# Sparse attention and a two-layer MLP on one core: scores and value products issued in runs per half unit, MLP matmuls pinned to their place, and the lower halves of weights subtracted on VectorE while weights are converted

## The chip, the core and the metric

The kernel runs on one core of a Trainium2 chip. The metric is the device time of one execution in microseconds, of which the median of three runs is taken. Five engines work side by side, each through its own list of instructions in order: TensorE (PE, whose weight loads are shown apart as PEld), VectorE (DVE), ScalarE (ACT), GpSimd (POOL) and SyncE (SP, here only an issuer of transfers).

## The reference

Three layers follow each other. Attention runs over 4 batches and 8 heads of 576 positions and 64 channels, where the first four heads see the last 32 positions and the others every 32nd position. Its output, 2304 tokens by 512, goes through an MLP with 2048 hidden units. The result is routed to eight experts of 288 tokens each by a greedy choice over all logits, and each expert is an MLP with 1024 hidden units.

```python
scores = scale * np.matmul(q, k.transpose(0, 1, 3, 2))
mask_local = (rel >= 0) & (rel < stride)
mask_strided = (rel >= 0) & (pos[None, :] % stride == pos[:, None] % stride)
attn = np.exp(scores - max); attn = attn / (attn.sum(-1) + 1e-09)
x = (attn @ v).transpose(0, 2, 1, 3).reshape(B * S, H * D)
...
h = x @ w_in
x = np.maximum(0.01 * h, h) @ w_out
...
logits = x @ w_gate        # greedy: each token one expert, each expert 288 tokens
out[mask] = np.maximum(x[mask] @ w1[e], 0.0) @ w2[e]
```

The weights `w_in` and `w_out` come as 64-bit floats and are made 32-bit on the chip.

## The kernel before

**Attention.** A unit is one batch and two heads; there are 16, each handled in two half units (`seq`, 32 in all). One turn of the loop in `attention()` works on three half units at once: the scores of the newest (`a_qk`, L147), the transposes of the weights of the one two turns older (`a_pt`, L185, in two parts), and the value products of the one three turns older (`a_pv`, L201); it also transposes q and k of the next unit (`a_tr`, L114). Two or three tiles make a half unit. The scores of a tile are two matmuls, one per head, each over 64 rows of the array (the two heads lie on different rows); the value products of a tile are two matmuls, each into 64 columns. A matmul of 32-bit floats shows as two records in the trace, so one tile of scores is an `x4` in a timeline.

**MLP.** Tokens are taken in six blocks of 384. A step `n` is one block and one of 16 slices of the hidden units. `g1` (L367) makes 12 matmuls of 384 columns, `g2` (L389) nine of 512 columns for the step before. Products of 32-bit floats are made from an upper and a lower half: `split` (L345) copies the weight slice into `hi`, and `lo` is the difference. In the matmuls `hi`/`lo` appear as operands of L374 to L376 and L398 to L400. The hidden values go through ScalarE (L382), VectorE (L383), ScalarE (L384) and VectorE (L385). The one bank `p1` that `g1` writes has a single buffer, so the first matmul of the next step (L374) waits until L383 has read it.

**Conversion.** `convert` (L313) turns a 512 KB piece of a 64-bit weight into 32 bits: ScalarE (L321), then three VectorE instructions (L323, L324, L325). The pieces are loaded from GpSimd's queue (L307, L310) into two buffers, each of which is loaded again when L325 has read it. There are 32 pieces, two per step of the first block.

**Order.** Each of the three is a Python generator; a `yield` marks where another may go on. `mlp()` asks before each step for what it needs: `2n + 3` converted pieces, and `DONE` half units of attention (8 for the first block, 16 for the second). Between its own yields, attention is advanced by a credit:

```python
            credit += 0.9 if DONE[0] < 16 else 0      # first 16 steps
        elif st < 64:
            credit += 0.5 if DONE[0] < 32 else 0
        ...
        while credit >= 1:
            next(A, None)
            credit -= 1
```

A list scheduler then orders each engine's instructions. It follows the program order as a priority and may move an instruction ahead; one on which `tc.keep_in_program_order` is called stays behind all that was written before it on its engine. In the kernel before, that call (`pin`) is used only in the expert part.

After step 47 three blocks have their second product left. These, the routing and the experts follow; the change does not touch them.

Of the kernel before, what the change touches and what calls it, by code (L numbers as in the profile page):

```python
# [26 lines left out]
def body(ctx, tc, q, k, v, w_in, w_out, w_gate, w1, w2, out):  # L27
# [119 lines left out]
    def a_qk(u, g):  # L147
        nq, nk, tl = group(u, g)
        n = len(tl)
        tag = "p2" if u < 5 and g else "pS"  # L150
        p = [ps.tile([128, 4, 128], F32, name=f"pS{h}", tag=tag, bufs=BUFS[tag]) for h in range(2)]
        s = at.tile([126, 2, 3, 128], F32, name="sc", tag="sc", bufs=3)
        mx = at.tile([126, 3, 2, 3], F32, name="mx", tag="mx", bufs=4)
        SC[u, g] = s, mx

        def score(i, m):
            for h in range(2):
                nc.vector.tensor_tensor_reduce(s[:nq, h, i, :nk], p[h][:nq, i, :nk], m[:nq, :nk], -0.125,  # L158
                                               3.0e38, OP.add, OP.min, mx[:nq, 0, h, i:i + 1])
                nc.scalar.activation(s[:nq, h, i, :nk], s[:nq, h, i, :nk], AF.Exp,  # L160
                                     bias=mx[:nq, 0, h, i:i + 1], scale=-1.0,
                                     accum_out=mx[:nq, 1, h, i:i + 1])

        for i, (q0, k0, m, _) in enumerate(tl):
            for h in range(2):
                r = slice(64 * h, 64 * h + 64)
                nc.tensor.matmul(p[h][:nq, i, :nk], QK[u][r, 0, 32 + q0:32 + q0 + nq],
                                 QK[u][r, 1, k0:k0 + nk], start=True, stop=True)
            if u < 2 and i:
                nc.tensor.matmul(p[0][:, 3], ident, QK[u][:, 0, 32:160], start=True, stop=True)  # L170
            yield
        for i, t in enumerate(tl):
            score(i, t[2])

# [10 lines left out]
    def a_pt(u, g, h):  # L185
        nq, nk, tl = group(u, g)
        n = len(tl)
        if h == 0:
            PT[u, g] = at.tile([128, 2, 3, 128], F32, name="pt", tag="pt")
        tag = "p2" if u < 5 and h else "pT"  # L190
        p = ps.tile([128, 4, 128], F32, name="pP", tag=tag, bufs=BUFS[tag])
        for _ in range(3 if u < 5 else 0):
            nc.tensor.matmul(p[:, 3], ident, ident, start=True, stop=True)
        for i in range(n):
            nc.tensor.transpose(p[:nk, i, :nq], SC[u, g][0][:nq, h, i, :nk], ident[:nq, :nq])
        if h or EARLY[0]:
            nc.scalar.activation(PT[u, g][:nk, h, :n, :nq], p[:nk, :n, :nq], AF.Copy)
        else:
            nc.vector.tensor_copy(PT[u, g][:nk, h, :n, :nq], p[:nk, :n, :nq])

    def a_pv(u, g):  # L201
        b, c = divmod(u, 4)
        nq, nk, tl = group(u, g)
        n = len(tl)
        t = PT.pop((u, g))
        tag = "p1" if u < 2 else "pT"
        p = ps.tile([128, 3 * 126], F32, name="pX", tag=tag, bufs=BUFS[tag])
        for i, tt in enumerate(tl):
            for h in range(2):
                nc.tensor.matmul(p[64 * h:64 * h + 64, i * nq:i * nq + nq], VT[u][:nk, tt[3], h, :],  # L210
                                 t[:nk, h, i, :nq], start=True, stop=True)
            if i == 0:
                yield
        pieces = []
        if c < 2:
            s0 = b * S + 288 * g
            o = 0
            while o < 288:
                j, a0 = divmod(s0 + o, BLK)
                w = min(288 - o, BLK - a0)  # L220
                pieces.append((p[:, o:o + w], *(x[:, c, a0:a0 + w] for x in xtile(j))))
                o += w
        else:
            r0, nr = 14 * g, n * nq // 18
            i0 = 0
            while i0 < 18:
                j, a0 = divmod(b * S + 32 * i0, BLK)
                i1 = min(18, i0 + (BLK - a0) // 32)
                pieces.append((p[:, :n * nq].rearrange("p (r i) -> p r i", i=18)[:, :, i0:i1],
                               *(x[:, c, a0:a0 + 32 * (i1 - i0)].rearrange("p (i r) -> p r i", r=32)[:, r0:r0 + nr]  # L230
                                 for x in xtile(j))))
                i0 = i1
        for src, dh, dl in pieces:
            (nc.scalar.copy if u else nc.vector.tensor_copy)(dh, src)
            nc.vector.tensor_sub(dl, src, dh.bitcast(F32))  # L235
# [4 lines left out]
    def attention():  # L240
# [9 lines left out]
        for s in range(n + 3):  # L250
            cur, mid, old = (seq[x] if 0 <= x < n else None for x in (s, s - 2, s - 3))
            u, g = cur or (99, 0)
            A = a_qk(u, g) if cur else iter(())
            V = a_pv(*old) if old else iter(())
            if u + 1 < 16 and s >= 1:
                a_tr(u + 1, g)
                yield
# [5 lines left out]
                yield  # L263
            if cur:
                next(A, None)
                yield
            if old:
                next(V)
                yield
            if u + 1 < 16 and g == 1:  # L270
                a_tr(u + 1, 2)
                yield
            if cur:
                next(A, None)
                yield
            if mid:
                a_pt(*mid, 1)
                yield
            for _ in A:
                pass  # L280
            if s < 1:
                a_tr(u + 1, g)
                yield
            if cur:
                a_norm(u, g)
            for _ in V:
                pass
            if old:
                DONE[0] += 1
            yield  # L290
            if g == 0 and u + 2 < 16:
                a_load(u + 2)
                v_load(u + 2)
# [51 lines left out]
    def split(pool, src, tag, n):  # L345
# [4 lines left out]
            nc.scalar.activation(hi, src, AF.Copy)  # L350
        else:
            nc.vector.tensor_copy(hi, src)  # L352
        nc.gpsimd.tensor_sub(lo, src, hi.bitcast(F32))  # L353
        return hi, lo


# [1 line left out]
    nc.gpsimd.memset(WB, 0.0)  # L358
    L = consts.tile([128, 18, 8], F32, name="L")
    SI, SO, GG, P2 = {}, {}, {}, {}  # L360

    def prep(n):

# [3 lines left out]
    def g1(n):  # L367
# [3 lines left out]
        p1 = ps.tile([128, BLK], F32, name="p1", tag="p1", bufs=1)  # L371
        for c in range(4):
            cs = slice(128 * c, 128 * c + 128)
            nc.tensor.matmul(p1, wh[:, cs], xh[:, c], start=(c == 0), stop=False)  # L374
            nc.tensor.matmul(p1, wh[:, cs], xl[:, c], start=False, stop=False)  # L375
            nc.tensor.matmul(p1, wl[:, cs], xh[:, c], start=False, stop=(c == 3))  # L376
            if c < 3:
                yield
# [10 lines left out]
    def g2(n):  # L389
# [5 lines left out]
        p2 = P2[blk]  # L395
        for t in range(3):
            s = slice(128 * t, 128 * t + 128)
            nc.tensor.matmul(p2[t], gh[:, s], oh, start=(f == 0), stop=False)  # L398
            nc.tensor.matmul(p2[t], gh[:, s], ol, start=False, stop=False)
            nc.tensor.matmul(p2[t], gl[:, s], oh, start=False, stop=(f == 15))  # L400
            if f == 15:
# [128 lines left out]
    A, Cv = attention(), conversion()  # L530
    bg = []
    for n, _ in enumerate(A):
        if n % 10 == 0:
            next(Cv, None)
        if DONE[0] >= 8:
            break
    credit = 0.0
    for n, _ in enumerate(mlp()):
# [3 lines left out]
        if st < 16:  # L542
            if n == 0:
                next(Cv, None)
            credit += 0.9 if DONE[0] < 16 else 0
        elif st < 64:
            credit += 0.5 if DONE[0] < 32 else 0
        if n == 20:
            for a in range(4):
                nc.sync.dma_start(WB[32 * a:32 * a + 32, :, 8 * a:8 * a + 8], w_gate.rearrange("(b j) e -> j b e", j=32))  # L550
# [138 lines left out]
            return f  # L689

    soon = Soon()

    def pin(x):

        tc.keep_in_program_order(x[0] if isinstance(x, tuple) else x)

    def search():

# [367 lines left out]
```

## Time and profile before

| | |
|---|---|
| time, median of 3 runs | 898.53 us (898.48 to 899.33) |
| the profiled execution | 891.85 us, of which 890.1 us is the span from first to last instruction |
| mean granted clock of TensorE | 0.978 of full speed |
| PE busy | 842.4 us (95% of the span) |
| DVE busy | 544.8 us (61%) |
| ACT busy | 441.5 us (50%) |
| POOL busy | 492.1 us (55%) |

The busy shares are averages over stages that differ. Three stretches matter here: up to 72.9 us attention runs almost alone; from 72.9 to 184.3 us steps 1 to 15 of the MLP run beside attention and conversion; from 184.3 to 374 us steps 16 to 47 run beside the rest of attention. PEclk is the granted share of TensorE's clock (1.00 is 2.4 GHz, 0.50 is 1.2 GHz).

### The profile page before, as it was taken

What the parts mean: (1) busy time and instruction counts of PE and PEld (TensorE: products, weight loads), DVE (VectorE), ACT (ScalarE), POOL (GpSimd) and SP (SyncE); (2) the same over time, 40 slices, a digit from 0 to 9 for tenths busy, and PEclk for the clock granted to TensorE, in tenths of its full rate; (3) what the DMA queues carried; (4) which work ended last, traced back from release to release, by engine and by line L of the source; (5) the groups of instructions that cost most, each with busy time, mean ns of one, the idle gap of its engine ahead of it and who ended that gap; (6) DMA issues with size and microseconds to landing.
All of it is one profiled execution on the core that took longest, in us unless ns stands there. A gap on an engine that the chain in (4) does not pass through costs nothing. (4 is left out here: it accounts for less than half of the span.)

```text
span 890.1 us, 17029 instructions
## 1 busy us (share of the span) xinstructions
PE 842.4 (95%) x6272; PEld 710.9 (80%) x6272; DVE 544.8 (61%) x1552; ACT 441.5 (50%) x1098; POOL 492.1 (55%) x402
## 2 busy tenths in 40 slices
PE   8799999899999999999999999997999999999994
PEld 5677766677777787788989777775899999899994
DVE  5787888865546565475645546454758878772320
ACT  5787667464546455444555323332544444444641
POOL 2655646564555565544645355575648547558731
PEclk8999989999999999999999999999899999999998
DMA  8587554420122000044000004362546445546510
GB/s 193 145 199 175 143 137 137 129 63 14 29 46 79 17 6 10 1 160 160 1 1 1 19 1 166 109 205 92 166 147 192 147 133 182 173 146 206 181 52 27
DMA packets 95411, 93.18 MB, mean 105 GB/s; under 512 B 66144, under 2 KB 74336, under 8 KB 95328
## 3 DMA queue, kind: packets, MB, share of 16 engines
q1 hardware_dynamic: 87648, 65.88, 26.0%
q0 software_dynamic: 7680, 26.22, 9.6%
q8 instruction: 49, 0.80, 0.4%
q14 instruction: 34, 0.28, 0.1%
HBM read 76.35 MB, written 15.73 MB: 103 GB/s over the span
## 5 line engine op out<-in xcount | busy, mean ns | idle before, releaser
L353 POOL TENSOR_TENSOR lo<-WI,hi 128x512 fp32r<-128x512 f32 x96 | 127.5, 1328 | 98.9 <-DVE hi L352 58.2
L353 POOL TENSOR_TENSOR lo<-WO,hi 128x512 fp32r<-128x512 f32 x96 | 125.9, 1312 | 88.3 <-ACT hi L350 88.1
L859 POOL TENSOR_TENSOR wlo<-raw,whi 128x1024 fp32r<-128x1024 f32 x48 | 116.8, 2445 | 26.7 <-ACT whi L858 21.7
L350 ACT ACTIVATE hi<-WO 128x512 fp32r<-128x512 f32 x96 | 60.6, 631 | 101.3 <-PE q L961 49.2
L374 PE MATMUL p<-xh,hi 128*128 128x384 f32 x192 | 75.7, 395 | 5.3 <-DVE g L383 5.3
L916 PE MATMUL g<-hh,whi 128*128 128x288 f32 x256 | 78.8, 308 | 0.4 <-DVE exl L879 0.4
L893 PE MATMUL g<-exh,whi 128*128 128x288 f32 x256 | 78.6, 308 | 0.0
L894 PE MATMUL g<-exl,whi 128*128 128x288 f32 x256 | 76.8, 301 | 0.0
L917 PE MATMUL g<-hl,whi 128*128 128x288 f32 x256 | 76.2, 298 | 0.4 <-DVE hl L901 0.4
L895 PE MATMUL g<-exh,wlo 128*128 128x288 f32 x256 | 76.3, 298 | 0.0
L918 PE MATMUL g<-hh,wlo 128*128 128x288 f32 x256 | 75.7, 296 | 0.0
L160 ACT ACTIVATE sc<-sc,mx 96x128 f32<-96x128 f32 (+2 forms) x176 | 67.6, 388 | 15.0 <-DVE mx L158 15.0
L858 ACT ACTIVATE whi<-raw 128x1024 fp32r<-128x1024 f32 x64 | 67.3, 1053 | 2.9 <-DMA raw<-in_moe_w_dram 2.9
L376 PE MATMUL p<-xh,lo 128*128 128x384 f32 x192 | 66.3, 345 | 1.4 <-POOL lo L353 1.2
L421 PE MATMUL p<-xh,hi 128*128 128x384 f32 x192 | 66.4, 346 | 0.0
L375 PE MATMUL p<-xl,hi 128*128 128x384 f32 x192 | 65.8, 343 | 0.2 <-DVE xl L235 0.2
L423 PE MATMUL p<-xh,lo 128*128 128x384 f32 x192 | 64.7, 337 | 0.7 <-POOL lo L353 0.7
L398 PE MATMUL p<-hi,gh 128*128 128x512 f32 x144 | 64.3, 446 | 0.7 <-ACT gh L384 0.7
L422 PE MATMUL p<-xl,hi 128*128 128x384 f32 x192 | 64.4, 335 | 0.0
L182 POOL TENSOR_TENSOR sc<-sc,mx 96x384 f32<-96x384 f32 (+2 forms) x64 | 52.2, 832 | 21.4 <-DVE mx L180 15.2
L932 POOL DMA_INDIRECT out_dram<-o,idx x24 | 24.3, 1011 | 70.4 <-ACT o L908 58.4
L400 PE MATMUL p<-hi,gl 128*128 128x512 f32 x144 | 57.4, 398 | 0.0
(210 smaller groups left out, 2294.3 us busy)
## 6 DMA issues: line engine op xcount, KB each, us to landing
raw<-in_moe_w_dram SPq DMA_DIRECT2D x64, 512.0 KB
wraw<-in_moe_w_in_dram POOLq DMA_DIRECT2D x16, 512.0 KB
wraw<-in_moe_w_out_dram POOLq DMA_DIRECT2D x16, 512.0 KB
g<-g3d SPq DMA_DIRECT2D x16, 384.0 KB
rawq<-in_q_dram SPq DMA_DIRECT2D x32, 144.0 KB
rawk<-in_k_dram SPq DMA_DIRECT2D x32, 144.0 KB
x2d<-x SPq DMA_DIRECT2D x18, 256.0 KB
g3d<-gh SPq DMA_DIRECT2D x16, 192.0 KB
```

The source lines that it names most:

```text
L160: nc.scalar.activation(s[:nq, h, i, :nk], s[:nq, h, i, :nk], AF.Exp, bias=mx[:nq, 0, h, i:i + 1], scale=-1.0, accum_out=mx[:nq, 1, h, i:i ...
L353: nc.gpsimd.tensor_sub(lo, src, hi.bitcast(F32))
L374: nc.tensor.matmul(p1, wh[:, cs], xh[:, c], start=(c == 0), stop=False)
L421: nc.tensor.matmul(p1, wh[:, cs], xh[:, c], start=(c == 0), stop=False)
L858: pin(nc.scalar.activation(hi, raw, AF.Copy))
L859: pin((nc.vector if n in (5, 7) else nc.gpsimd).tensor_sub(lo, raw, hi.bitcast(F32)))
L893: nc.tensor.matmul(p, wh, xh[:, c], start=(c == 0), stop=False)
L894: nc.tensor.matmul(p, wh, xl[:, c], start=False, stop=False)
L895: nc.tensor.matmul(p, wl, xh[:, c], start=False, stop=(c == 3))
L916: nc.tensor.matmul(p, wh, hh[:, j], start=(j == 0), stop=False)
L917: nc.tensor.matmul(p, wh, hl[:, j], start=False, stop=False)
L918: nc.tensor.matmul(p, wl, hh[:, j], start=False, stop=(j == 7))
```

## The change

In `a_qk` the `yield` after each tile of scores goes: one turn issues the scores of all tiles of a half unit in one go. In `a_pv` the `yield` after the first tile goes as well, so all its value products come in one go. The loop of `attention()` loses the yields between these parts: from 8 or 9 per turn it comes to 5 or 6, and the credits are scaled with that (0.9 to 0.6, 0.5 to 0.33), as is the rate of conversions ahead of the MLP (every 10th yield to every 6th). `pin` is moved up and called on the first matmul of each group of three in `g1` and `g2`. The lower half in `split` is subtracted on VectorE until the last piece is converted (`CONV[0] > 31`), and on GpSimd after. The banks tagged `p2` are lent to attention for units 0 to 3 rather than 0 to 4.

```diff
@@ a_qk
-        tag = "p2" if u < 5 and g else "pS"
+        tag = "p2" if u < 4 and g else "pS"
...
             if u < 2 and i:
                 nc.tensor.matmul(p[0][:, 3], ident, QK[u][:, 0, 32:160], start=True, stop=True)
-            yield
+        yield
         for i, t in enumerate(tl):
             score(i, t[2])
@@ a_pt
-        tag = "p2" if u < 5 and h else "pT"
+        tag = "p2" if u < 4 and h else "pT"
@@ a_pv
-            if i == 0:
-                yield
@@ attention
-            V = a_pv(*old) if old else iter(())
...
             if cur:
                 next(A, None)
-                yield
             if old:
-                next(V)
+                a_pv(*old)
+                DONE[0] += 1
                 yield
...
-            if cur:
-                next(A, None)
-                yield
...
-            for _ in A:
-                pass
...
-            for _ in V:
-                pass
-            if old:
-                DONE[0] += 1
-            yield
@@ split
-        nc.gpsimd.tensor_sub(lo, src, hi.bitcast(F32))
+        (nc.gpsimd if CONV[0] > 31 else nc.vector).tensor_sub(lo, src, hi.bitcast(F32))
@@ g1
-            nc.tensor.matmul(p1, wh[:, cs], xh[:, c], start=(c == 0), stop=False)
+            pin(nc.tensor.matmul(p1, wh[:, cs], xh[:, c], start=(c == 0), stop=False))
@@ g2
-            nc.tensor.matmul(p2[t], gh[:, s], oh, start=(f == 0), stop=False)
+            pin(nc.tensor.matmul(p2[t], gh[:, s], oh, start=(f == 0), stop=False))
@@ body
-        if n % 10 == 0:
+        if n % 6 == 0:
...
-            credit += 0.9 if DONE[0] < 16 else 0
+            credit += 0.6 if DONE[0] < 16 else 0
...
-            credit += 0.5 if DONE[0] < 32 else 0
+            credit += 0.33 if DONE[0] < 32 else 0
```

How this moves instructions is seen in the built order of each engine, which holds no times. On PE, early in the MLP (step 4), the scores of one half unit of the strided heads (three tiles, `pS_1238` and `pS_1239`; written at L167) stand between pieces of `g2` (L398 to L400) in the kernel before:

```order
L167 MATMUL pS_1238<-qk 108x108
L167 MATMUL pS_1239<-qk 108x108
L398 MATMUL p_1056<-hi,gh 128x512
L399 MATMUL p_1056<-lo,gh 128x512
L400 MATMUL p_1056<-hi,gl 128x512
L195 MATMUL pP<-ident,sc 128x96 x3
L398 MATMUL p_1057<-hi,gh 128x512
L399 MATMUL p_1057<-lo,gh 128x512
L400 MATMUL p_1057<-hi,gl 128x512
L167 MATMUL pS_1238<-qk 108x108
L167 MATMUL pS_1239<-qk 108x108
L398 MATMUL p_1058<-hi,gh 128x512
```

In the changed kernel, whose lines past the first edit are 2 to 13 lower (L398 is L389), the same half unit stands so:

```order
L390 MATMUL p_1055<-lo,gh 128x512
L391 MATMUL p_1055<-hi,gl 128x512
L167 MATMUL pS_1251<-qk 108x108
L167 MATMUL pS_1252<-qk 108x108
L167 MATMUL pS_1251<-qk 108x108
L167 MATMUL pS_1252<-qk 108x108
L167 MATMUL pS_1251<-qk 108x108
L167 MATMUL pS_1252<-qk 108x108
L389 MATMUL p_1056<-hi,gh 128x512
```

Two of the three tiles are seen in the first fence, apart from each other, and the third stood later still; the three are now one run.

On PE at the turn to step 3, the value products (L210) of a half unit of the local heads in the kernel before:

```order
L210 MATMUL pX<-pt,vt 64x96 x2
L398 MATMUL p_1057<-hi,gh 128x512
L399 MATMUL p_1057<-lo,gh 128x512
L400 MATMUL p_1057<-hi,gl 128x512
L398 MATMUL p_1058<-hi,gh 128x512
L399 MATMUL p_1058<-lo,gh 128x512
L400 MATMUL p_1058<-hi,gl 128x512
L195 MATMUL pP<-ident,sc 128x96 x3
L374 MATMUL p_1185<-xh,hi 128x384
L375 MATMUL p_1185<-xl,hi 128x384
L376 MATMUL p_1185<-xh,lo 128x384
L210 MATMUL pX<-pt,vt 64x96 x4
```

and in the changed one:

```order
L365 MATMUL p_1176<-xh,hi 128x384
L366 MATMUL p_1176<-xl,hi 128x384
L367 MATMUL p_1176<-xh,lo 128x384
L210 MATMUL pX<-pt,vt 64x96 x6
L365 MATMUL p_1176<-xh,hi 128x384
```

The two matmuls, and the four that stood three groups of matmuls behind them, are one run of six.

On VectorE around the hidden values of step 4 (`g<-p_1286`, L383), the kernel before has conversion (L323 to L325), the hidden values (L383, L385), and attention (L136, L179, L180, L235):

```order
L323 TENSOR_SCALAR cg<-cg 128x512
L324 SCALAR_TENSOR_TENSOR cg<-wraw,cg 128x512
L383 TENSOR_TENSOR g<-p_1286,g 128x384
L325 SCALAR_TENSOR_TENSOR WO<-wraw,cg 128x512
L179 TENSOR_SCALAR mx<-mx 108x6
L136 COPY qk<-pT 128x192
L385 TENSOR_TENSOR gl<-g,gh 128x384
L180 RECIPROCAL mx<-mx 108x6
```

The changed one has at the same place (`g<-p_1279`, now L374; conversion is L310 to L312):

```order
L340 TENSOR_TENSOR lo<-WO,hi 128x512
L311 SCALAR_TENSOR_TENSOR cg<-wraw,cg 128x512
L312 SCALAR_TENSOR_TENSOR WI<-wraw,cg 128x512
L179 TENSOR_SCALAR mx<-mx 108x6
L180 RECIPROCAL mx<-mx 108x6
L233 TENSOR_TENSOR xl<-pX,xh 128x192
L374 TENSOR_TENSOR g<-p_1279,g 128x384
L233 TENSOR_TENSOR xl<-pX,xh 128x96
L340 TENSOR_TENSOR lo<-WI,hi 128x512
L376 TENSOR_TENSOR gl<-g,gh 128x384
L310 TENSOR_SCALAR cg<-cg 128x512
L136 COPY qk<-pT 128x192
```

The lower halves (L340) of `WO` and `WI` have come in, one ahead of the step's hidden values and one behind them. In the whole order 31 of the 192 subtractions of `split` are on VectorE, four of them ahead of the hidden values of step 0; the same place has 12 conversions behind it instead of 10.

## Rows read from the trace of the kernel before

**Rows 1.** Busy time by engine in three stretches, with granted clock and DMA share.

```profile
0.00:72.90 72.90, 61.53 (x520) 48.31 (x520) 51.66 (x224) 52.81 (x195) 36.15 (x51) 0.93 0.75 180
72.90:184.30 111.40, 103.27 (x631) 76.57 (x630) 94.15 (x215) 71.57 (x209) 65.09 (x68) 0.95 0.50 134
184.30:374.00 189.70, 189.70 (x1365) 149.51 (x1365) 103.51 (x338) 99.02 (x299) 104.09 (x93) 1.00 0.12 31
```

**Rows 2.** Matmuls grouped by line and shape, 72.9 to 184.3 us.

```profile
L374 PE MATMUL p<-xh,hi 128*128 128x384 f32 x60 | 25.2, 420 | 5.3 <-DVE g L383 5.3
```

**Rows 3.** Timeline of PE around one tile of scores: start us, length us.

```profile
297.50 0.39 PE L399 MATMUL p<-lo,gh 128*128 128x512 f32 x1
297.73 0.39 PE L400 MATMUL p<-hi,gl 128*128 128x512 f32 x1
298.05 0.46 PE L167 MATMUL pS<-qk 64*96 64x128 f32 x4
298.44 0.50 PE L398 MATMUL p<-hi,gh 128*128 128x512 f32 x1
298.78 0.39 PE L399 MATMUL p<-lo,gh 128*128 128x512 f32 x1
```

**Rows 4.** Timeline of PE, a run of scores ahead of the MLP.

```profile
53.77 1.34 PE L167 MATMUL pS<-qk 64*96 64x128 f32 x20
55.04 0.71 PE L193 MATMUL pP<-ident 128*128 128x128 f32 x4
```

**Rows 5.** Timeline of PE, four tiles' and two tiles' records of value products.

```profile
301.20 0.59 PE L210 MATMUL pX<-pt,vt 108*64 108x108 f32 x8
301.73 0.44 PE L374 MATMUL p<-xh,hi 128*128 128x384 f32 x1
...
309.87 0.39 PE L210 MATMUL pX<-pt,vt 128*64 128x96 f32 x4
310.18 0.50 PE L398 MATMUL p<-hi,gh 128*128 128x512 f32 x1
```

**Rows 6.** VectorE instructions grouped by line and shape, 72.9 to 184.3 us.

```profile
L324 DVE SCALAR_TENSOR_TENSOR cg<-wraw,cg 128x512 int32<-128x512 int32 x22 | 24.3, 1106 | 0.3
L323 DVE TENSOR_SCALAR cg<-cg 128x512 int32<-128x512 int32 x21 | 17.4, 828 | 6.4 <-ACT cg L321 6.4
L325 DVE SCALAR_TENSOR_TENSOR WO<-wraw,cg 128x512 int32<-128x512 int32 x11 | 10.5, 953 | 0.1
...
L325 DVE SCALAR_TENSOR_TENSOR WI<-wraw,cg 128x512 int32<-128x512 int32 x11 | 9.4, 858 | 0.2
```

**Rows 7.** Timeline of all engines around one wait of step 7.

```profile
113.47 0.42 DVE L323 TENSOR_SCALAR cg<-cg 128x512 int32<-128x512 int32 x1
...
113.92 0.69 DVE L324 SCALAR_TENSOR_TENSOR cg<-wraw,cg 128x512 int32<-128x512 int32 x1
...
114.46 1.28 POOL L353 TENSOR_TENSOR lo<-WI,hi 128x512 fp32r<-128x512 f32 x1
114.65 1.64 DVE L325 SCALAR_TENSOR_TENSOR WI<-wraw,cg 128x512 int32<-128x512 int32 x1
...
116.21 0.55 DVE L383 TENSOR_TENSOR g<-p,g 128x384 f32<-128x384 f32 x1
...
116.81 0.44 PE L374 MATMUL p<-xh,hi 128*128 128x384 f32 x1 [1.66 <-DVE g L383]
```

**Rows 8.** GpSimd instructions grouped by line and shape, 72.9 to 184.3 us.

```profile
L353 POOL TENSOR_TENSOR lo<-WI,hi 128x512 fp32r<-128x512 f32 x16 | 22.3, 1397 | 5.9 <-ACT hi L350 5.7
L353 POOL TENSOR_TENSOR lo<-WO,hi 128x512 fp32r<-128x512 f32 x14 | 19.3, 1378 | 4.1 <-ACT hi L350 4.0
L307 POOL DMA_DIRECT2D wraw<-in_moe_w_in_dram x10 | 7.9, 793 | 18.0 <-DVE WI L325 7.1 <-PE pX L210 3.1 <-DVE gl L385 2.7
L182 POOL TENSOR_TENSOR sc<-sc,mx 96x384 f32<-96x384 f32 x8 | 6.4, 824 | 1.8 <-DVE mx L180 1.8
```

**Rows 9.** Waits of PE, 0 to 72.9 us: total us, times, longest us.

```profile
PE pP L193 <- ACT qk L134: 2.2, 2, 1.5
```

More of the change, by code (lines that the diff above doesn't have):

```diff
@@ L360, in body, with pin @@
     SI, SO, GG, P2 = {}, {}, {}, {}
+    def pin(x):
+        tc.keep_in_program_order(x[0] if isinstance(x, tuple) else x)
     def prep(n):
@@ L691, in body @@
     soon = Soon()
-    def pin(x):
-        tc.keep_in_program_order(x[0] if isinstance(x, tuple) else x)
     def search():
```

## The prediction

> **What bounds the kernel now.** I first cut the span into stretches by step and read the busy time of each engine [rows 1]. From 184.3 to 374 us PE is busy for 189.70 of 189.70 us at full clock, and VectorE for 103.51: there PE's own order is the bound, and time taken off PE is time taken off the end. From 72.9 to 184.3 us PE is busy for 103.27 of 111.40 and VectorE for 94.15, the most of the others, and the granted clock is 0.95. This stretch holds 15 steps, since L374 runs four times in each and 60 times in all [rows 2]; it has 7.4 us per step, the next stretch of 32 steps 5.9, though conversion and not matmuls is what the first has more of. PE waits there for VectorE's L383, 5.3 us [rows 2]. In the first 72.9 us VectorE has 51.66 us of work and 21 us idle [rows 1].
>
> Then I asked what a piece of attention costs between matmuls of the MLP. L399 to L400 takes 0.23 us from start to start, and this is what a full matmul of 512 columns holds PE for. Where one tile of scores stands between, L400 to the second matmul behind the tile takes 298.78 - 297.73 = 1.05 us, so the tile costs 1.05 - 2 x 0.23 = 0.59 [rows 3]. Of it some 0.09 is ahead of the tile and 0.11 behind the first matmul after it (0.34 instead of 0.23). In a run, 20 records, which are five tiles, take 55.04 - 53.77 = 1.27 us, or 0.25 a tile [rows 4]. So a break into 64-row matmuls and back costs 0.59 - 0.25 = **0.34 us**, whatever it holds. Value products: two tiles (four records) take 0.31 us to the next matmul, four records more take 0.53, that is 0.22 for what was added [rows 5]; with 0.09 and 0.11 as above, a break costs 0.31 + 0.20 - 0.22 = **0.29 us**.
>
> Last I read why VectorE is so busy. The same L324 takes 0.69 us at 113.92 and 1.11 in the mean of 22; L325 takes 1.64 at 114.65, where GpSimd's L353 runs from 114.46 to 115.74, and VectorE goes on only after that. L383 comes at 116.21, and PE has waited 1.66 us for it [rows 6, 7]. Over the stretch the four groups hold 24.3 + 17.4 + 10.5 + 9.4 = 61.6 us; at 0.69 for L324 and L325 and 0.42 for L323 they would need 44 x 0.69 + 21 x 0.42 = 39.2. So **22.4 us** of VectorE's busy time is standing behind GpSimd.
>
> **The change, part by part.**
>
> *Runs from step 16 on.* By the built orders, scores stand in 32 runs before and 13 after, value products in 32 and 16. That removes 19 x 0.34 + 16 x 0.29 = 11.1 us of PE. Some attention slips here from the steps before 16 (three tiles of scores at 0.25, and transposes): I estimate 1.5 us. PE is the bound, so the end moves by **-9.6 us**. Bounds: if only the 0.11 behind a run is saved, 35 x 0.11 - 1.5 = 2.4; if a tile in a run costs 0.20, 12.
>
> *Runs in steps 1 to 15.* 22 to 9 runs of scores, 15 to 8 of value products: 13 x 0.34 + 7 x 0.29 = 6.4 us less on PE, and the 1.5 that slipped.
>
> *Lower halves on VectorE.* GpSimd loses 16 + 14 subtractions, 22.3 + 19.3 = 41.6 us, and keeps the L182s, 16 in the same view at 0.8 us, or 12.8 [rows 8]. If VectorE stands behind GpSimd in proportion, 22.4 x 41.6 / 54.4 = 17.1 us go. What comes in is 27 subtractions (31 less the four ahead of step 0). No row has one on VectorE. L324 reads two operands of the same 128x512, and without disturbance takes 0.69 [rows 7]; at the top stands 1.64, an L325 behind GpSimd. I take 0.69, since GpSimd has little left to stand behind: 18.6 us in. Two conversions more lie ahead of step 0, 2 x (0.42 + 0.69 + 0.69) = 3.6 us out. VectorE's sum is 94.15 - 17.1 + 18.6 - 3.6 = 92, hardly less than before. What changes is that no instruction ahead of L383 lasts 3 us, and that the pieces' loads, which GpSimd issues between its subtractions, go out earlier; VectorE's L323 waits 6.4 us for what those loads feed [rows 6].
>
> *The stretch.* PE needs 111.40 less 5.3 of waits, less 0.05 x 111.4 = 5.6 of half clock, less 6.4 and 1.5: 92.6 us, as much as VectorE. Two engines at 92 that wait for each other don't reach 92. VectorE is busy for 85% now; with its idle of 17 us cut by the waits for L321 and some others it should come to 89%, which is 103.4 us: **-8 us**. Bounds: at 94% it is 98, or -13; at 80%, if the subtractions wait for ScalarE's `hi` with everything queued behind them (conversion, L383, and so PE), 115, or +4.
>
> *Ahead of step 1.* Two conversions and four subtractions, 3.6 + 2.8 = 6.4 us, enter VectorE's first 72.9 us, which have 21 idle; if that cover is gone, the MLP starts 6.4 us later. Scores reach VectorE one piece earlier. I take **+1 us**, between -2 and +6.
>
> *Pins, credits, banks.* The pin adds no instruction. The credits give 4.2 yields a step at 5.5 a half unit where 6.3 at 8.5 stood, which is 3% faster; attention is not what the end waits for. Attention gives back the `p2` banks one unit earlier, as `g2` wants them. I count these at nothing; what a bad pin would cost is a rival.
>
> *Sum:* -9.6 - 8 + 1 = -16.6 us. The rows come from an execution of 891.85 us, which would become 875. It is 6.7 us under the median of the runs, and I take the difference off the median: 898.53 - 16.6 = **882 us**.
>
> **Rivals.**
>
> *VectorE takes it back.* Its sum in steps 1 to 15 is the same, and the new subtractions wait for `hi` in line. Then the stretch gains nothing, and the start loses 2: 898.5 - 9.6 + 2 = 891. For it: 94 of 111 us are busy already. Against: a quarter of this is standing still, which goes. The Trainium skill (Perfetto Trace Analysis, Optimizing Scalar/DVE Operations) says that moving work between GpSimd and VectorE might not help, as they share a read port. The trace agrees that one stands behind the other [rows 7]; by the rule this case would be the likeliest.
>
> *The stretch becomes PE's.* It falls to 95 us, the clock stays up, -16: 898.5 - 9.6 - 16 = 873. For it: most of PE's waits stand behind blocked instructions. Against: VectorE would need 97%.
>
> *Loads are held up.* VectorE gets 27 more instructions with two operands; if each of the 20 loads that GpSimd issues in the stretch is held up by one of 0.69 us, 13.8 us, of which half is on the path as two buffers alternate, 889. Against: the issue of L307 takes 793 ns in the mean of 10 though VectorE is busy for 85% of that time [rows 1, 8]. The Trainium skill (SBUF — State Buffer, SBUF: two separate sides) says that a transfer issued from GpSimd starves while VectorE holds the shared port in a two-port mode, and has one go from some 620 to some 3100 ns. By that the issues would differ widely; the trace doesn't show it [rows 8].
>
> *The pins cost more than the runs save (slower).* An MLP group can no longer pass an attention piece whose operand is late. Place: the first matmul of a score run, which needs both `pS` banks and the copy of q and k, or of a `pT` piece that needs the bank two pieces back. Where no MLP stands between, such a wait took up to 1.5 us [rows 9]. About 22 half units come after step 0; 16.6 us of gain are gone at 0.75 us for each, and at 1 us the time is 898.5 - 16.6 + 22 = 904. Against: from 184.3 us on PE waits for nothing [rows 1], and two turns of the loop lie between the scores of a half unit and their transposes.
>
> *Breaks don't cost what they seem to* (the runs drain as the tiles did): -2.4 and nothing else, 896.
>
> **Chances.** The forecast 0.49, with its own range 874 to 889; VectorE takes it back 0.20; PE's stretch 0.12; loads 0.04; pins 0.12; breaks 0.03. Below 870 lies half of PE's case, above 896 the pins' and some of VectorE's with a late start: 870 to 896 leaves out some 0.19. A change of under 0.2%, or 1.8 us, is about what a measurement of this kernel can't tell from none. Faster: the first four less 0.04, and breaks: 0.83. Same 0.05, slower 0.12.
>
> **What would show it.** After step 16, PE still busy throughout, 5.6 us or less a step, and score records as x8 and x12. In steps 1 to 15, L324 near 0.7 us in the mean, lower halves on VectorE near 0.69, fewer and shorter waits for L383's counterpart, clock above 0.95. The prediction is wrong if the subtractions wait for ScalarE at length, if step 1 starts past 76 us, or if PE waits inside attention pieces.

## The result, and the profile after

The changed kernel takes **884.33 us** (median of 4 runs, 880.87 to 887.44) where the kernel before takes 898.5 (897.41 to 899.33): ratio 0.9845, interval 0.982 to 0.987. The profiled execution lasted 884.1 us, of which 882.3 us is the span. Lines of kernel.py lie 2 to 13 lower than before: L374 became L365, L383 L374, L324 L311, L353 L340, L321 L308.

Busy time by engine, in the same three stretches as [rows 1] (to step 1, steps 1 to 15, steps 16 to 47; then PE, PEld, VectorE, ScalarE, GpSimd, granted clock, DMA share, GB/s):

```profile
0.00:86.30 86.30, 73.66 (x519) 56.19 (x519) 54.61 (x228) 55.35 (x199) 29.39 (x48) 0.82 0.67 159
86.30:186.40 100.10, 90.02 (x603) 71.79 (x602) 87.93 (x237) 68.65 (x202) 28.84 (x39) 1.00 0.55 142
186.40:367.00 180.60, 180.60 (x1398) 151.58 (x1397) 105.33 (x346) 100.98 (x299) 103.29 (x93) 1.00 0.13 32
```

Step 1 starts at 86.3 us instead of 72.9: **+13.4**. Steps 1 to 15 take 100.1 us instead of 111.4: **-11.3**. Steps 16 to 47 take 180.6, from 184.3 to 374.3 before 190.0: **-9.4**. What follows takes 882.3 - 367.0 = 515.3 instead of 890.1 - 374.3 = 515.8. The sum is -7.8 us, the difference of the two profiled executions.

VectorE's groups in steps 1 to 15, for [rows 6] (busy us, mean ns | idle before them, and what ended it), and PE's first matmul of a group, for [rows 2]:

```profile
L311 DVE SCALAR_TENSOR_TENSOR cg<-wraw,cg 128x512 int32<-128x512 int32 x20 | 16.4, 820 | 0.4
L340 DVE TENSOR_TENSOR lo<-WI,hi 128x512 fp32r<-128x512 f32 x14 | 9.8, 703 | 0.6 <-ACT hi L337 0.5
L340 DVE TENSOR_TENSOR lo<-WO,hi 128x512 fp32r<-128x512 f32 x13 | 9.5, 733 | 0.5 <-ACT hi L337 0.4
L310 DVE TENSOR_SCALAR cg<-cg 128x512 int32<-128x512 int32 x20 | 9.5, 476 | 7.3 <-ACT cg L308 7.3
...
L312 DVE SCALAR_TENSOR_TENSOR WO<-wraw,cg 128x512 int32<-128x512 int32 x10 | 7.3, 730 | 0.1
L312 DVE SCALAR_TENSOR_TENSOR WI<-wraw,cg 128x512 int32<-128x512 int32 x10 | 6.9, 688 | 0.1
...
L365 PE MATMUL p<-xh,hi 128*128 128x384 f32 x60 | 22.8, 381 | 5.7 <-DVE g L374 4.0 <-ACT hi L337 1.7
```

The four conversion groups need 16.4 + 9.5 + 7.3 + 6.9 = 40.1 us where they took 61.6. The 27 lower halves bring 19.3, at 703 and 733 ns. The subtractions hardly wait for ScalarE's `hi`: 0.5 and 0.4 us. PE, though, stands no less in this stretch: 100.10 - 90.02 = 10.1 us where it stood 111.40 - 103.27 = 8.1. Its waits for `g` went only from 5.3 us [rows 2] to 4.0, and 1.7 us for `hi` came in. What fell is its busy time, by 13.3 us, with the granted clock at 1.00 where it was 0.95.

PE around a run of scores and one of value products, both of the steps from 16 on (start, length), for [rows 3, 5]:

```profile
209.61 0.40 PE L391 MATMUL p<-hi,gl 128*128 128x512 f32 x1
209.93 0.71 PE L167 MATMUL pS<-qk 64*126 64x126 f32 x8
210.57 0.50 PE L389 MATMUL p<-hi,gh 128*128 128x512 f32 x1
210.91 0.40 PE L390 MATMUL p<-lo,gh 128*128 128x512 f32 x1
...
214.60 0.39 PE L391 MATMUL p<-hi,gl 128*128 128x512 f32 x1
214.92 0.72 PE L210 MATMUL pX<-pt,vt 128*64 128x96 f32 x12
215.56 0.50 PE L389 MATMUL p<-hi,gh 128*128 128x512 f32 x1
215.90 0.39 PE L390 MATMUL p<-lo,gh 128*128 128x512 f32 x1
```

Two tiles of scores in one run cost 210.91 - 209.61 - 2 x 0.23 = 0.84 us, worked out as for [rows 3]; apart they cost 2 x 0.59 = 1.18. That is 0.34 saved for one break, with tiles of 126 columns here and 128 there. Three tiles of value products also cost 0.84; as x8 and x4 they cost, by the prediction's reading of [rows 5], 0.53 + 0.20 and 0.31 + 0.20, or 1.24. That is 0.40 for one break, and a little too much, since the x8 read there has 108 columns and these have 96.

One place where attention falls behind on the way to step 1 is at 36 to 41 us. The timelines of GpSimd, ScalarE and PE in the kernel after:

```profile
35.58 0.58 POOL L297 DMA_DIRECT2D wraw<-in_moe_w_out_dram  x1
...
39.52 0.67 ACT L308 ACTIVATE cg<-wraw 128x512 f32<-128x512 f32 x1 [2.57 <-DMA wraw<-in_moe_w_out_dram]
40.09 0.70 ACT L197 ACTIVATE pt<-pP 128x288 f32<-128x288 f32 x2
...
40.55 0.39 PE L123 MATMUL pT<-ident,rawq 96*128 96x96 f32 x2 [3.29 <-ACT pt L197]
```

and of the kernel before:

```profile
37.97 0.59 POOL L310 DMA_DIRECT2D wraw<-in_moe_w_out_dram  x1
...
43.99 0.67 ACT L321 ACTIVATE cg<-wraw 128x512 f32<-128x512 f32 x1
```

In the kernel after, ScalarE reaches a conversion (L308) before the raw weights are there and stands 2.57 us; the copy `pt` is queued behind it, and PE stands 3.29 us for the bank that this copy frees. Before, the load was issued later, but ScalarE came to the conversion 6 us behind the issue and didn't wait. Summed up to step 1 (us, times, longest), after:

```profile
ACT cg L308 <- DMA wraw<-in_moe_w_out_dram: 5.6, 3, 2.6
...
PE pT L123 <- ACT pt L197: 3.7, 2, 3.3
```

and before:

```profile
PE pT L123 <- ACT pt L197: 2.0, 2, 1.5
...
ACT cg L321 <- DMA wraw<-in_moe_w_in_dram: 0.8, 2, 0.4
```

PE stood behind that copy before, too, 2.0 us in all, so what this place shows is a part of the 13.4 us and not the whole. In the whole stretch up to step 1, PE is busy for 12.1 us more than before with as many matmuls (73.66 for 61.53 us, 519 for 520 in the rows), at a clock of 0.82 instead of 0.93, and stands 1.3 us more.

### The profile page after: what moved, and what is told of

The parts are those of the page before. It is cut to its first block, busy times and chain, and to the rows that moved or that the text cites. A ratio compares the mean times of both kernels' runs of the same rounds, so it can differ in the third digit from the quotient of the medians.

```text
span 882.3 us, 17050 instructions
## 1 busy us (share of the span) xinstructions
PE 831.7 (94%) x6272; PEld 717.2 (81%) x6272; DVE 543.4 (62%) x1584; ACT 443.0 (50%) x1097; POOL 449.6 (51%) x371
## 5 line engine op out<-in xcount | busy, mean ns | idle before, releaser
L340 POOL TENSOR_TENSOR lo<-WI,hi 128x512 fp32r<-128x512 f32 x80 | 105.2, 1316 | 90.5 <-DVE hi L339 58.2
L340 POOL TENSOR_TENSOR lo<-WO,hi 128x512 fp32r<-128x512 f32 x81 | 104.5, 1290 | 79.6 <-ACT hi L337 79.5
L365 PE MATMUL p<-xh,hi 128*128 128x384 f32 x192 | 72.7, 378 | 5.7 <-DVE g L374 4.0
L882 PE MATMUL g<-exh,wlo 128*128 128x288 f32 x256 | 77.1, 301 | 0.0
L412 PE MATMUL p<-xh,hi 128*128 128x384 f32 x192 | 66.2, 345 | 0.0
L389 PE MATMUL p<-hi,gh 128*128 128x512 f32 x144 | 61.4, 427 | 0.0
```

The costliest lines, as they stand in the source:

```text
L340: (nc.gpsimd if CONV[0] > 31 else nc.vector).tensor_sub(lo, src, hi.bitcast(F32))
L365: pin(nc.tensor.matmul(p1, wh[:, cs], xh[:, c], start=(c == 0), stop=False))
L882: nc.tensor.matmul(p, wl, xh[:, c], start=False, stop=(c == 3))
```

## The experiments

The theories: **1**, the start is late because step 0's matmuls, pinned, no longer stand between attention, and TensorE's clock falls; **2**, VectorE's extra conversions and subtractions delay it; **3**, the scores' work stands too early in ScalarE's and VectorE's queues; **4**, banks are lent for one unit less; **5**, whole runs expose latency; **6**, the half clock itself makes it late. The table has the profiled execution of each kernel, cut at the first matmul of steps 1, 16 and 48 (L365, in step 48 L412, or their counterparts), and the runs against the kernel before, which took 895.2 us beside e0 to e3, 896.2 beside e4 to e7 and 896.9 beside e8 to e11.

| kernel | step 1 at | steps 1-15 | steps 16-47 | step 48 at | median us | ratio to before |
|---|---|---|---|---|---|---|
| before | 72.9 | 111.4 | 190.0 | 374.3 | 898.5 | 1 |
| after | 86.3 | 100.1 | 180.6 | 367.0 | 884.33 | 0.9845 (0.982-0.987) |
| e0_before_again | 73.3 | 111.6 | 189.9 | 374.8 | 894.34 | 0.9988 (0.9969-1.0007) |
| e1_no_pin | 83.9 | 106.6 | 178.6 | 369.1 | 884.09 | 0.9872 (0.9849-0.9895) |
| e2_subs_gpsimd | 82.8 | 114.4 | 180.6 | 377.8 | 893.21 | 0.9977 (0.9959-0.9994) |
| e3_conv10 | 81.5 | 104.8 | 179.0 | 365.3 | 881.1 | 0.9833 (0.9802-0.9864) |
| e4_subs_only | 78.3 | 102.4 | 190.1 | 370.8 | 892.81 | 0.9958 (0.9936-0.998) |
| e5_scores_late | 80.3 | 104.0 | 178.2 | 362.5 | 878.59 | 0.9793 (0.9764-0.9822) |
| e6_split_early | 83.5 | 104.6 | 178.0 | 366.1 | 882.1 | 0.9822 (0.9784-0.9859) |
| e7_lend5 | 81.6 | 89.0 | 218.0 | 388.6 | 906.73 | 1.0119 (1.0086-1.0151) |
| e8_after_again | 86.1 | 100.0 | 180.6 | 366.7 | 885.06 | 0.9873 (0.9839-0.9906) |
| e9_fill_six | 84.6 | 100.1 | 180.7 | 365.4 | 882.29 | 0.9854 (0.9821-0.9886) |
| e10_late_pin1 | 77.0 | 103.1 | 179.2 | 359.3 | 876.95 | 0.979 (0.976-0.9819) |
| e11_late_conv10 | 77.1 | 107.3 | 182.1 | 366.5 | 885.59 | 0.9886 (0.9859-0.9912) |

Attention that is done in one stretch is missing in the next (PE's instruction counts in the rows differ), so where two columns move against each other, the place of step 48 is what counts.

**e0_before_again**: the kernel before, unchanged.

> The kernel before once more, unchanged, with a second profile. The profiled execution shown above lasted 891.85 us, 6.7 us under the median of 898.53. If the difference lies between the executions, this profile comes near 898 and the stretches by step show where 6.7 us come and go (most likely where the granted clock falls to half). If it lies in the profiling, it comes near 892 again. Ratio to itself 1.00.

The profiled execution took 891.05 us, and the stretches came out within 0.4 us of the first profile. Executions of this kernel lie between 888.96 and 897.81 us in these runs, the shortest three at a granted clock of 0.983 to 0.985, the longest two at 0.978 and 0.975. By the mark that I had set, a profile near 892 again speaks for the profiling as the cause of the 6.7 us; but executions of 888.96 and 890.14 us came without a profile, so executions do differ by as much. Which of the two it was stays open.

**e1_no_pin**

```diff
-            pin(nc.tensor.matmul(p1, wh[:, cs], xh[:, c], start=(c == 0), stop=False))
+            nc.tensor.matmul(p1, wh[:, cs], xh[:, c], start=(c == 0), stop=False)
...
-            pin(nc.tensor.matmul(p2[t], gh[:, s], oh, start=(f == 0), stop=False))
+            nc.tensor.matmul(p2[t], gh[:, s], oh, start=(f == 0), stop=False)
```

> The changed kernel without the two pins: first matmuls of a group may again move ahead of attention pieces. Theory 1 (the start is late because PE has only attention ahead of step 1: with step 0's matmuls no longer between it, the granted clock falls to half for 17 us): step 0's matmuls stand between attention again, the half-clock time ahead of step 1 falls below 10 us, step 1 starts 8 to 13 us earlier than in the changed kernel (at 73 to 78 us), and the time falls by up to 10 us, to 874 to 880, unless later steps lose it. Theory 2 (VectorE's two conversions and four subtractions more): start stays at 84 to 87 us, time within 3 us of the changed kernel's 884.

Step 0's first matmul stands at 52.0 us again, between attention, but step 1 starts at 83.9 and the time is the same. Theory 1 fails as the main cause: taking the pins out wins 2.4 us of the start, and nothing of the time.

**e2_subs_gpsimd**

```diff
-        (nc.gpsimd if CONV[0] > 31 else nc.vector).tensor_sub(lo, src, hi.bitcast(F32))
+        nc.gpsimd.tensor_sub(lo, src, hi.bitcast(F32))
```

> The changed kernel with every lower half on GpSimd again, as in the kernel before; runs, pins and the pace of conversion as changed. If the lower halves are what shortened steps 1 to 15 (100.1 us against 111.4), the stretch is back at 106 to 112 us, with L365's first matmul waiting for VectorE's g, and the time is 889 to 896. If the runs shortened it, it stays at 100 to 103 and the time near 884. If the four subtractions ahead of step 0 are what makes the start late (theory 2), step 1 starts 3 us or more earlier than 86.3; by theory 1 it starts at 85 to 87 as before.

Of the 14.2 us, 2 are left. In the profile, steps 1 to 15 and steps 16 to 47, then groups of steps 1 to 15:

```profile
82.80:197.20 114.40, 95.45 (x608) 76.97 (x609) 96.83 (x204) 70.64 (x205) 64.41 (x66) 0.94 0.46 126
197.20:377.80 180.60, 180.60 (x1399) 151.59 (x1398) 104.97 (x346) 100.94 (x299) 102.25 (x92) 1.00 0.13 32
```

```profile
L310 DVE TENSOR_SCALAR cg<-cg 128x512 int32<-128x512 int32 x20 | 20.5, 1023 | 6.2 <-ACT cg L308 6.2
L311 DVE SCALAR_TENSOR_TENSOR cg<-wraw,cg 128x512 int32<-128x512 int32 x20 | 19.8, 991 | 0.4
...
L365 PE MATMUL p<-xh,hi 128*128 128x384 f32 x61 | 24.9, 408 | 10.6 <-DVE g L374 10.5
```

L310 is back at 1023 ns, with GpSimd busy for 64 of 114 us, where it takes 476 with GpSimd busy for 29 of 100, and PE waits 10.5 us for `g`. The lower halves decide this stretch; it is 14.3 us longer without their move. Steps 16 to 47 keep their 180.6 us: that gain is not the lower halves'. The start moves by 3.5 us, so the four early subtractions carry a part of theory 2.

**e3_conv10**

```diff
-        if n % 6 == 0:
+        if n % 10 == 0:
```

> The changed kernel with a conversion at every tenth yield ahead of the MLP instead of every sixth, which puts 11 instead of 12 conversions ahead of step 0's g. Theory 2 (VectorE's conversions make the start late): step 1 starts 2 to 6 us earlier, at 80 to 84 us. Theory 1: it starts within 1.5 us of 86.3, and the time stays within 3 us of 884.

Step 1 starts 4.8 us earlier, as theory 2 has it, but step 48 stands only 1.7 us earlier: most is given back in steps 1 to 15, where the conversion is then done (and 86 records of scores run there instead of 76). The time is 881.1, about 3 us under the changed kernel.

**e4_subs_only**: the kernel before with one edit.

```diff
-        nc.gpsimd.tensor_sub(lo, src, hi.bitcast(F32))
+        (nc.gpsimd if CONV[0] > 31 else nc.vector).tensor_sub(lo, src, hi.bitcast(F32))
```

> The kernel before with one edit alone: lower halves on VectorE while weights are converted. Runs, pace of conversion, lent banks and order as before. If the lower halves alone shorten steps 1 to 15, as the profile of the changed kernel with GpSimd's subtractions suggests (100.1 against 114.4 us), that stretch falls from 111.4 to 98 to 104 us, step 1 starts at 73 to 77 us, steps 16 to 47 stay at 190, and the time is 884 to 890 where the kernel before takes 895. If the gain needs the runs as well (rival: VectorE takes it back), the stretch stays above 108 us and the time within 3 us of before.

```profile
0.00:78.30 78.30, 63.88 (x529) 49.27 (x530) 54.16 (x230) 55.28 (x205) 29.73 (x47) 0.93 0.72 172
78.30:180.70 102.40, 97.53 (x613) 73.61 (x612) 90.17 (x247) 70.69 (x204) 31.51 (x40) 0.98 0.54 142
180.70:370.80 190.10, 190.10 (x1378) 149.78 (x1376) 102.75 (x329) 98.32 (x291) 103.26 (x93) 1.00 0.12 31
```

The windows by step: steps 1 to 15 fall by 9.0 us without any run, so "VectorE takes it back" falls. Steps 16 to 47 stay at 190.1. With e2 this separates the two terms: -9.4 belongs to the runs and what came with them (pins, credits, banks), with the lower halves and without. The time (892.81) misses the range expected, since the start rose by 5.4 us, though the clock up to step 1 is 0.93 as before; PE has 529 records there for 520, so a small part of it is attention done earlier. Here too ScalarE stands for raw weights ahead of step 1, 4.7 us for those of the second matrix:

```profile
ACT cg L321 <- DMA wraw<-in_moe_w_out_dram: 4.7, 4, 2.2
```

**e5_scores_late**

```diff
-            if cur:
-                next(A, None)
             if old:
                 a_pv(*old)
...
             if cur:
+                next(A, None)
                 a_norm(u, g)
```

> The changed kernel with one call moved: the VectorE and ScalarE work on a half unit's scores is written behind the second transposes, as in the kernel before, instead of ahead of the value products. Theory 3 (the start is late because that work now stands in ScalarE's and VectorE's queues ahead of the copies that PE waits for): step 1 starts 4 us or more before the 86.3 us of the changed kernel, and the pieces of attention at 45 to 55 us lose their lag of 4 us. Theory 4 (the start is late because a bank pair lent one unit less makes unit 4 wait at about 60 us) and theory 5 (it is the whole runs that expose latency where no MLP stands between): start within 2 us of 86.3.

Step 1 starts 6.0 us earlier, step 48 4.5 us earlier, and the time is 878.59: the order of the scores' work matters, as theory 3 says. Its second mark failed: attention at 45 to 55 us is as late as in the changed kernel, and the 6 us are won between 60 and 80 us.

**e6_split_early**: runs only from the twelfth half unit on.

```diff
-        yield
+            if split:
+                yield
+        if not split:
+            yield
...
+            split = s < 11
-            A = a_qk(u, g) if cur else iter(())
+            A = a_qk(u, g, split) if cur else iter(())
+            V = a_pv(*old, split) if old else iter(())
...
-        if n % 6 == 0:
+        if n % 10 == 0:
```

> The changed kernel with the attention ahead of the MLP written as in the kernel before (scores and value products split, ten yields per conversion), and as changed from the twelfth half unit on; lent banks as changed. Theory 5 or 3: step 1 starts at 73 to 78 us, the half clock ahead of it is gone, and with steps 1 to 15 at 100 to 106 us the time is 873 to 880. Theory 4 (banks): step 1 still starts past 82 us, with PE waiting at about 60 us, and the time is 881 to 886.

Neither: step 1 starts at 83.5 us though attention ahead of it is written as before, and the time is 882.1. Theory 5 fails as a main cause. Ahead of the MLP this kernel is written as e4 but for the pins and the lent banks (the smaller credit and the runs come behind that), and its step 1 starts 5.2 us later: that much comes on top of the lower halves' 5.4.

**e7_lend5**: e1 with the banks lent for one unit more.

```diff
-        tag = "p2" if u < 4 and g else "pS"
+        tag = "p2" if u < 5 and g else "pS"
...
-        tag = "p2" if u < 4 and h else "pT"
+        tag = "p2" if u < 5 and h else "pT"
```

> The changed kernel without its pins and with the p2 banks lent for five units again; compared with the kernel without pins alone (step 1 at 83.9 us, 884.1 us). Theory 4 (the bank pair lent one unit less makes unit 4 wait and the clock fall at about 60 us): step 1 starts at 74 to 79 us, clock in 60 to 80 us above 0.9 where it was 0.76 and 0.56, time 875 to 880. Theories 3 and 5: start at 82 to 85, time within 3 us of 884.

Slower than before: 906.73 us, 22.6 above e1. Step 1 starts at 81.6, so theory 4 fails for the start. But attention then stops. The matmuls of value products in 76 to 182 us, and the one step from 170.6 to 212.4:

```profile
L210 PE MATMUL pX<-pt,vt x48: 246/256/420, 76.3 to 180.1; 128*64 128x96 f32 x36, 108*64 108x108 f32 x12
...
busy tenths in 40 slices 0002000300000000000000000000000000000000
```

```profile
170.60:212.40 41.80, 34.74 (x262) 25.14 (x262) 17.94 (x100) 27.29 (x105) 12.66 (x17) 0.76 0.32 77
```

Two short pieces of value products run at 84.5 and 94.9 us, and then none until 177.6 (a slice is 22.6 us). That unit 4's pieces wait for `p2` banks that the MLP now holds until its first block is done is the reading, from the edit and the place where they go on; no row names it. Six of the steps between, from 105.9 to 133.0 us, take 4.2 to 5.4 us, and the attention left over takes 41.8 us in one. So the edit that I counted at nothing is needed by the others. With the pins this was not tried.

**e8_after_again**: the changed kernel, unchanged.

> The changed kernel once more, with a second profile. If the half clock ahead of step 1 belongs to the kernel, the granted clock up to step 1 is again below 0.86 and step 1 starts at 83 to 88 us; if it was this one execution, the clock is 0.9 or more and step 1 starts before 80. Time 882 to 886.

```profile
0.00:86.10 86.10, 69.53 (x520) 53.52 (x520) 55.48 (x234) 56.02 (x201) 29.39 (x48) 0.87 0.69 169
```

```profile
75.65 0.34 PE L367 MATMUL p<-xh,lo 128*128 128x384 f32 x1
77.83 1.65 PE L193 MATMUL pP<-ident 128*128 128x128 f32 x6 [1.84 <-ACT qk L134]
79.27 0.69 PE L195 MATMUL pP<-ident,sc 96*128 96x96 f32 x3
79.66 0.67 PE L365 MATMUL p<-xh,hi 128*128 128x384 f32 x1
```

The same start, 86.1 us, at another clock: 0.87 where the first profile had 0.82, with PE busy 69.5 us where it was 73.7. What the clock gave back, PE stood. The timeline shows one such wait inside step 0: a transposes piece waits 1.84 us for ScalarE, and the pinned matmul of step 0 stands behind it.

**e9_fill_six**

```diff
-        for _ in range(3 if u < 5 else 0):
+        for _ in range(6 if u < 5 else 0):
```

> The changed kernel with six instead of three matmuls of the identity ahead of the transposes of the first five units (30 more matmuls of 128 columns ahead of step 1, some 0.06 us each at full clock, most of it while PE would stand). Theory 6 (PE stands, the clock falls to half, and the matmuls ahead of step 1 take twice as long: PE is busy 73.7 us up to step 1 for the 61.5 of before, with as many matmuls): with less standing the clock up to step 1 rises from 0.82 to 0.88 or more, step 1 starts at 78 to 83 us, time 878 to 882. Rival (the start waits for a chain through ScalarE and VectorE, and the clock only follows): step 1 starts at 86 to 89 us whatever the clock, time 884 to 888.

```profile
0.00:84.60 84.60, 72.83 (x612) 59.93 (x612) 60.33 (x229) 55.26 (x195) 31.65 (x50) 0.94 0.74 179
```

The clock up to step 1 rises to 0.94, above that of the kernel before, and the start moves by 1.7 us. That lies between what theory 6 and its rival gave (78 to 83, 86 to 89), and the run can't decide between them, since the added matmuls did not go into PE's idle time. PE's records of L193 up to step 1, in the changed kernel and here:

```profile
L193 PE MATMUL pP<-ident 128*128 128x128 f32 x114 | 21.1, 328 | 2.0 <-ACT qk L134 1.3 <-ACT pt L197 0.7
...
L193 PE MATMUL pP<-ident 128*128 128x128 f32 x216 | 31.4, 292 | 3.9 <-ACT qk L134 2.1 <-DVE xl L233 1.2 <-ACT pt L197 0.7
```

They take 10.3 us more (the expectation counted 30 matmuls at 0.06 us). PE is busy for 72.8 us where it was 73.7 and stands 11.8 us where it stood 12.6: what the clock gave back, the added matmuls used up. VectorE is busy for 60.3 us instead of 54.6 as well, with 14 pieces converted ahead of step 1 instead of 12. What the start would be at full clock without such work stays open.

**e10_late_pin1**: e5, and step 0 not pinned.

```diff
-            pin(nc.tensor.matmul(p1, wh[:, cs], xh[:, c], start=(c == 0), stop=False))
+            x = nc.tensor.matmul(p1, wh[:, cs], xh[:, c], start=(c == 0), stop=False)
+            if n >= 1:
+                pin(x)
```

> Scores written late as in the version at 878.6 us, and step 0's matmuls not pinned, so that they may stand between attention ahead of step 1. If the pin on step 0 costs the start what step 0 takes, 6 us, step 1 starts at 74 to 77 us instead of 80.3 and the time is 873 to 876; if those 6 us are paid somewhere else, it starts at 78 to 82 and the time stays within 2 us of 878.6.

Start 77.0 us, 3.3 of the 6 us expected; step 48 at 359.3, 3.2 earlier than in e5; the time is 876.95, the least of all, though its interval overlaps that of e5. ScalarE stands 6.1 us for raw weights ahead of step 1 here (5.2 and 0.9 for the two matrices), more than the 5.6 of the changed kernel, and step 1 is 9.3 us earlier: this wait alone doesn't set the start. Steps 16 to 47 in this kernel:

```profile
180.10:359.30 179.20, 179.20 (x1379) 150.43 (x1380) 104.81 (x344) 101.23 (x301) 104.25 (x93) 1.00 0.13 33
```

They hold 128 records of scores and 156 of value products, as many as in the kernel before; the changed kernel has 140 and 156.

**e11_late_conv10**: e5, and the edit of e3.

> Scores written late as in the version at 878.6 us, and one conversion fewer ahead of the MLP (every tenth yield). If the two edits add up (the one took 5.7 us off the changed kernel's time, the other 3), step 1 starts at 75 to 78 us and the time is 874 to 877; if both only kept the clock from falling at the same place, it stays at 877 to 880.

The start is as expected, 77.1 us, and ScalarE stands there for raw weights only 0.6 us. The time is not: 885.59. Steps 1 to 15 take 107.3 us, and PE stands once more in the next stretch, behind VectorE:

```profile
PE p L390 <- DVE gl L375: 2.4, 1, 2.4
```

An early start that leaves conversion undone is paid for later.

## Why the prediction was right, and where it was not

The time (882 forecast, 884.33 and 885.06 measured) came out by terms of which two held and one failed.

*Runs from step 16 on*, -9.6: measured **-9.4**, in two pairs of kernels (after against before, e2 against before; e4 has no runs and 190.1). The break of a run of scores is 0.34 us, as priced; that of value products up to 0.40 instead of 0.29. PE issues 33 instructions more in this stretch (1398 for 1365), of which 22 are attention that slipped in, 12 of them scores. e10 tells the two apart as far as they can be: with no scores slipped, PE still busy throughout, it takes 179.2 us, -10.8 for the 11.1 forecast of the breaks alone, and the 1.4 us from there to the changed kernel's 180.6 are near the 1.5 estimated for the slip.

*Steps 1 to 15*, -8: measured **-11.3**, and by its own steps. The standing of VectorE went (61.6 to 40.1 us, with 20 conversions for 21 or 22), the lower halves brought 19.3 us for 18.6 forecast, VectorE's sum is 87.9 for 92, its busy share 88% for 89. L311 kept some of it, 820 ns in the mean. One sign failed: PE's waits for `g` fell by a quarter only, and PE stands 10.1 us for 8.1. Its busy time came to 90.0 us where I had summed 92.6. The runs did not shorten this stretch by themselves: e2, which has them, takes 114.4 us, and beside the lower halves they bring 2.3 (102.4 to 100.1), not the 6.4 us of PE that I subtracted for them. The Trainium skill (Perfetto Trace Analysis, Optimizing Scalar/DVE Operations) warns that moving work between GpSimd and VectorE might not help. Here it helped: the trace shows that one stands behind the other [rows 7], and e4 that moving the lower halves alone brings -9.0 us.

*Ahead of step 1*, +1, between -2 and +6: measured **+13.4** and, in the second pair of profiles, 86.1 - 73.3 = +12.8. This is the step that failed, by the mark that I had set (past 76 us). I priced VectorE's added 6.4 us against its 21 idle us, and the pins and banks at nothing. VectorE was not full there, busy for 54.6 of 86.3 us, and the start moved all the same. Put in one after another, the lower halves alone move it by 5.4 us (e4), pins and banks, with the smaller credit, by 5.2 more (e6 against e4), and runs, place of the scores' work and pace of conversion by the 2.8 left (the changed kernel against e6). Undone singly, every edit gives a part and none the whole: pins 2.4 us, early subtractions 3.5, conversion pace 4.8, place of the scores' work 6.0. The first three don't bring the time down in proportion. Which share of the 13 us is whose stays open, since the parts hide one another.

How the edits do it is shown in part. Queues that work in turn come to things that are not ready: ScalarE stands 5.6 us for raw weights, PE behind its copies, step 0 behind PE's transposes. But e10 has as much of the first and starts at 77.0. And by PE's account most of the added time is not standing: it is busy 12.1 us longer at a clock of 0.82 instead of 0.93, and stands 1.3 us more; in the second pair (e8, e0) it is busy 7.7 us longer and stands 5.1 more. Whether the half clock held the start up, or only filled time in which step 1 would have waited anyhow, no run settles. My rival of late loads looked at the same loads, but in steps 1 to 15 and with VectorE's instructions holding up their issue; here the load at 36 us was issued 2.4 us earlier than before, and ScalarE came to it sooner still.

*Pins, credits, banks*, 0: right for the pins in the time (e1: 884.09 us), not for the start (above). For the banks the sum was right only because the edit was made; without it the kernel without pins loses 22.6 us (e7).

*The rivals.* VectorE did not take it back (e4), and breaks cost what they seemed to. The stretch went less than half the way to PE's case: 100.1 us, between 103.4 and 95. PE does wait inside attention pieces in steps 1 to 15, 2.5 us for `qk` ahead of transposes and some 1.8 in others, but without the pins the time is the same.

*The offset.* I took the sum off the median, 6.7 us above the profiled execution. The profiles differ by 7.8 us (second pair 6.4), the medians by 14.2 and 11.8. Both profiles of before are of short executions, at a clock of 0.978 and 0.983, while the others go down to 0.974; where those lose their time no trace here shows. The changed kernel has no such offset: its profiled execution took 884.1 us, its median is 884.33. Against the 875 that the sum gave for the profiled execution it is 9 us late. So the total was met by luck: an error of +12 us at the start was made good by the offset and by a stretch better by 3.

*Slips in the working.* Three things are off, and none of them moves the forecast. Four records of value products are one tile and not two [rows 5]; the price goes by records and stands. The upper bound of 12 for the runs leaves out the 1.5 us that the lower one takes off. The chances of faster add up to 0.84, not 0.83.

## What to carry to other kernels

Don't price a moved instruction by how many idle microseconds its new engine has: VectorE had 21 of them ahead of step 1, and moving the lower halves there, without any other edit, made step 1 5.4 us later (e4). Look at what stands behind it in the queues. Where two engines stand behind each other, moving the short form of the work to the faster one may pay even if its busy time falls little (94.2 to 90.2 us in e4, for a stretch shorter by 9.0). Where a stretch starts earlier, look at the place of a later step before counting a gain: of 4.8 us won at step 1, 1.7 were left at step 48.

## What was unexpected of the hardware

Two executions of the changed kernel reached step 1 within 0.2 us of each other at granted clocks of 0.82 and 0.87: in the second PE was busy 4.1 us less and stood 3.9 us more. The same subtraction of two 128x512 operands takes 0.70 to 0.73 us on VectorE and 1.38 to 1.40 on GpSimd [rows 8], and with these on GpSimd, VectorE's one-operand L310 rises from 476 to 1023 ns (e2).
